# Talking-heads attention, then a Fourier mix with feed-forward: the last Fourier parts placed behind the first feed-forward products

## The chip, the cores and the metric

The kernel runs on one core of one Trainium2 chip. The metric is the device time of one execution in microseconds, median of several runs. Names used below: TensorE (PE, matrix products; its weight load is listed as PEld), VectorE (DVE), ScalarE (ACT), GpSimd (POOL), SyncE (SP, which here only issues transfers). SBUF is the on-chip memory, PSUM the accumulators of TensorE. Each engine works through its own instructions in order and waits where data or a buffer is not ready.

## The reference, cut to what matters

```python
# attention: batch 8, 12 heads, 448 rows, head size 64
scores = scale * np.matmul(q, k.transpose(0, 1, 3, 2))
scores = np.einsum('bhij,hg->bgij', scores, w_pre)      # heads mixed
scores = scores - np.max(scores, axis=-1, keepdims=True)
attn = np.exp(scores)
attn = attn / (np.sum(attn, axis=-1, keepdims=True) + 1e-09)
attn = np.einsum('bhij,hg->bgij', attn, w_post)         # heads mixed again
attn_out = np.matmul(attn, v)
# bridge: (B,H,S,D) -> (B, S, H*D) = (8, 448, 768)
X = np.fft.fft(np.fft.fft(x, axis=1), axis=2)
u = x + np.real(X)
un = (u - mean(u)) / np.sqrt(var(u) + 1e-06)            # over the last axis
ch = np.maximum(un @ w_ch1, 0.0) @ w_ch2                # 768 -> 3072 -> 768
out = u + ch
```

## The kernel before, where it is touched

**Two phases.** `mix_phase` does attention and the Fourier mix batch by batch. Its loop counts steps `s`; a batch has 24 of them, eight batches 192. `ffn_phase` does norm and feed-forward over seven tiles of 512 rows (`t`), for six column blocks of the weights (`c`). One pair (c, t) is called a unit here: `first` makes seven products of w1 (a fast two-by-two scheme with seven instead of eight products), `second` seven of w2. Tile 0 holds the rows of batch 0 and the beginning of batch 1.

**The Fourier mix of a batch** comes behind its attention. `emit_x` turns the attention's output into rows X. `fold` makes sums and differences of pairs of rows on GpSimd. `emit_z` transforms along the rows (TensorE, then a ScalarE copy into z), four times a batch. `emit_s2` transforms along the columns and VectorE adds the result to X, four times a batch. Then `store` writes X to two arrays in DRAM, one of them in reversed order by an indirect transfer. The places of these steps, counted from the batch's first step, run to 55, so for the last batch they lie behind step 192:

```python
AT_X = (11, 20, 24, 29)
AT_Z = (38, 38, 41, 41)
AT_S = ((40, 44), (53, 55))
...
    with tc.manual_schedule(engines={ET.PE, ET.DVE, ET.Activation, ET.Pool}):
        while s < TOT or any(fill.values()):
            ...
            if 0 <= s < TOT:
                emit_turn(s)
            if s >= 4:
                wts.deal(1)
            ...
            for _ in range(min(len(folds), 1 if n and s > 3 else 2)):
                folds.pop(0)()
            take("full", s)          # X, z and s2 that are due
            s += 1
        flush()
        while later:
            later.pop(0)()           # stores
        wts.deal(1000)
```

**The weights** are given as 64-bit numbers. `_Weights` loads a piece raw, rebuilds 32-bit numbers with seven VectorE operations, makes the sums of the fast scheme and stores them. `deal(n)` puts n of these operations into the program. The load of a piece's first raw weight is an operation of its own that counts as none, and the first `deal` of the kernel is that of step 4.

```python
        self.ops.append((lambda: load(k0 + self.ahead - 1), False))
        for k in range(len(ps)):
            self.ops.append((lambda k=k: begin(k), True))
            ...
    def deal(self, n):
        while self.later:
            self.later.pop(0)()
        while self.ops and (n > 0 or not self.ops[0][1]):
            fn, dve = self.ops.pop(0)
            fn()
            n -= dve
```

**The feed-forward phase** begins with its own pools, the loads, the norm of tile 0, and then the units:

```python
    for i in ORDER:
        load_w1(0, i)
    for t in range(2):
        load_u(t)
    for x in range(NT2):
        stats(0, x)              # VectorE
    power(0)                     # four small GpSimd operations: (var + eps) ** -0.5
    for x in range(NT2):
        norm(0, x)               # ScalarE
        turn(0, x)               # six transposes on TensorE, two ScalarE copies
    for n in range(4):
        total(0, n)              # sums for the fast scheme, VectorE
    for i in ORDER:
        load_w2(0, i)
    with tc.manual_schedule(engines={mybir.EngineType.PE, mybir.EngineType.DVE}):
        for n in range(NC * NTB):
            c, t = divmod(n, NTB)
            if c + 1 < NC and t < NK + FM:
                wts.add(c + 1, t)
            wts.deal(0)
            if c == 0 and t + 2 < NTB:
                load_u(t + 2)
            second(n, first(n))
            wts.deal(1000)
```

Its PSUM tiles are two of kind Q and three each of kinds P and R[...].

Of the kernel before, what the change touches and what calls it, by code (L numbers as in the profile page):

```python
# [10 lines left out]
F32 = mybir.dt.float32  # L11
# [270 lines left out]


@with_exitstack
def mix_phase(ctx, tc, ident, q, k, v, w_pre, w_post, u_scr, u_rev, wts):

# [2 lines left out]

    def pool(name, bufs=1, **kw):
        return ctx.enter_context(tc.tile_pool(name=name, bufs=bufs, **kw))

    praw = pool("praw", 4)
    pqt = pool("pqt", 4)
# [4 lines left out]
    psm = pool("psm", 4)  # L301
    ppv = pool("ppv", 2)
    pxt = pool("pxt")
    pxx = pool("pxx", 6)
    pxs = pool("pxs")
    pxf = pool("pxf")
    pzz = pool("pzz")
    wts.open(ctx, tc)
    cst = pool("cst")
    pmx = pool("pmx", space=bass.MemoryType.PSUM)  # L310
# [13 lines left out]
    def room(n):  # L324
        if sum(e[0] for e in pend) + n > 4:
            flush()

    def ms_tile():
        return pms.tile([P, 512], F32, name="ms", tag="ms")


    cn = {n: nc.inline_tensor(a, name="k_" + n) for n, a in _consts().items()}
# [25 lines left out]
                kw2[:, :, r:30:R], wrp[:, 1, :].rearrange("p (y g) -> p y g", y=2),  # L358
                mk[:, 1, r:r + 1], None, op0=ALU.mult)

    rows = cst.tile([PN, 2], U32, name="rows")
    ts = cst.tile([PN, 2, 2, PN], F32, name="ts")
    tcs = cst.tile([CW, 2, 2, 2, DQ + 1], F32, name="tcs")

    def emit_tables():
        for t, n in ((rows, "at"), (ts, "ts"), (tcs, "tc")):
# [312 lines left out]
    def due(kind, at, fn):  # L679
        fill[kind].append((at, len(fill[kind]), fn))  # L680
# [5 lines left out]
    for b in range(B):  # L686
        f = b * GS
        at_t = [(a, nm, xx) for xx, at in enumerate(AT_T) for nm, a in zip("qk", at)]
        for at, (a, nm, xx) in zip(AT_L, sorted(at_t, key=lambda e: e[0])):
            loads.append(f + a - GS)  # L690
            for y in range(2):
                due("none", f + at[y] - GS,
                    lambda b=b, xx=xx, nm=nm, y=y: emit_load_qk(b, xx, nm, y))
        for xx, at in enumerate(AT_T):
            for nm, a in zip("qk", at):
                due("full", f + a - GS, lambda b=b, xx=xx, nm=nm: emit_xpose(b, xx, nm))
        for pr in range(3):
            for y in range(2):
                due("none", f + AT_V[pr][y], lambda b=b, pr=pr, y=y: emit_load_v(b, pr, y))
        for n in range(2 * NG):  # L700
            for xx in range(3):
                due("QK", f + BS * n - 7 + AT_QK[n][xx],
                    lambda n=2 * NG * b + n, xx=xx: (emit_qk(n, xx), n))
        for n in range(NG):
            g = groups[b * NG + n]
            for pr in range(3):
                due("AV", f + GT * (n + 1) + AT_AV[n][pr],
                    lambda g=g, pr=pr: (emit_av(g, pr), None))
            due("full", f + AT_X[n], lambda g=g: emit_x(g))
        for n, at in enumerate(AT_Z):  # L710
            due("full", f + at, lambda b=b, n=n: emit_z(b, n // 2, n % 2))
        for pair in range(2):
            for par in range(2):
                due("full", f + AT_S[pair][par],
                    lambda b=b, pair=pair, par=par: emit_s2(b, pair, par))
    due("none", max(loads[:6]) - 6, emit_load_mix)
    due("none", -3, emit_mix)
    due("none", 3, emit_tables)
# [18 lines left out]
    s = int(min(v_[0][0] for v_ in fill.values()))  # L737
    ET = mybir.EngineType
    with tc.manual_schedule(engines={ET.PE, ET.DVE, ET.Activation, ET.Pool}):
        while s < TOT or any(fill.values()):  # L740
            old = len(later)
            n = take("none", s)
            if 0 <= s + LM < TOT:
                emit_premix(s + LM)
            flush()
            if 0 <= s < TOT:
                emit_postmix(s)
            if 0 <= s + LM < TOT:
                emit_max(s + LM)
                emit_exp(s + LM)  # L750
            take("AV", s)
# [4 lines that stand above are left out]
            take("QK", s)  # L756
            if 0 <= s + LG < TOT:
                if any(e[2] is not None and e[2] <= (s + LG) // BS for e in pend):
                    flush()
                emit_gather(s + LG)  # L760
            if 0 <= s + LM < TOT:
                emit_scale(s + LM)
            for _ in range(old):
                later.pop(0)()
            for _ in range(min(len(folds), 1 if n and s > 3 else 2)):
                folds.pop(0)()
            take("full", s)
            s += 1
        flush()
        while later:  # L770
            later.pop(0)()
        wts.deal(1000)

# [10 lines left out]


@with_exitstack
def ffn_phase(ctx, tc, ident, u_scr, u_rev, wts, ub_scr, out):

    nc = tc.nc

    def pool(name, bufs=1, **kw):
        return ctx.enter_context(
            tc.tile_pool(name=name, bufs=bufs, reuse_waits="tile", **kw))

    pw1 = pool("pw1", 7)
    pub = pool("pub", 11)
    pun = pool("pun", 2)
# [1 line left out]
    ph = pool("ph")  # L801
    pst = pool("pst", 4)
    wts.open(ctx, tc, 2)
    pu = pool("pu")
    pps = pool("pps", space=bass.MemoryType.PSUM)

    NT2 = TB // P
    HT = TB // 2

    def ps_tile(key):  # L810
        return pps.tile([P, 512], F32, name="ps" + key, tag="ps" + key,
                        bufs=2 if key == "Q" else 3)

    us, ubs, w1, w2 = {}, {}, {}, {}
    mhalf = pst.tile([P, NT2], F32, name="mhalf", bufs=1)
    nc.gpsimd.memset(mhalf[:, :], -0.5)

    def load_u(t):
        us[t] = pu.tile([P, NT2, DM], F32, name=f"u{t}", tag=f"u{t}")
        for x in range(NT2):  # L820
            p = 0
            while p < P:
                b, r = divmod(t * TB + x * P + p, S)
                k = sum(r >= e for e in ENDS)
                n = min(P - p, ENDS[k] - r)
                src = (u_rev if k % 2 else u_scr)[b]
                for p0, m in _split(p, n):
                    nc.sync.dma_start(out=us[t][p0:p0 + m, x, :],
                                      in_=src[r + p0 - p:r + p0 - p + m, :])
                p += n  # L830
# [61 lines left out]
    def first(n):  # L892
# [7 lines left out]
        for k, i in enumerate(ORDER):  # L900
# [27 lines left out]
            if norms and k < NT2:  # L928
                stats(t + 1, k)
                if k == NT2 - 1:  # L930
                    power(t + 1)
            if i != 2:
                wts.deal(2 if norms else 3)
            if t == NTB - 1 and c + 1 < NC:
# [10 lines left out]
    def second(n, h):  # L945
# [9 lines left out]
        for k, i in enumerate(ORDER):  # L955
            for x in range(NT2 // 2):
                if i in OPENS:
                    ps[ACC[i], x] = ps_tile(ACC[i])
                p = ps[ACC[i], x][:, :DH]
                for kf in range(FM):  # L960
                    nc.tensor.matmul(p, lhs[i][:, kf, x * P:(x + 1) * P],  # L961
                                     w2[i][:, kf, :], start=i in OPENS and kf == 0,
                                     stop=kf == FM - 1, skip_group_check=True)
                for r, d in {0: [(0, 0)], 1: [(0, 0)], 4: [(1, 1)], 5: [(0, 1)],
                             2: [(0, 1)], 6: [(1, 1)], 3: [(1, 0)]}[i]:
                    us_ = u[:, 2 * r + x, d * DH:(d + 1) * DH]
                    nc.vector.tensor_tensor(us_, us_, p, op=ALU.add)  # L967
                    if c == NC - 1 and i in (1, 6, 2, 3):
                        r0 = t * TB + (2 * r + x) * P
                        nc.sync.dma_start(out=out[r0:r0 + P, d * DH:(d + 1) * DH],  # L970
                                          in_=us_)
            if i == 1:
                nc.vector.tensor_tensor(h12, h12, hs2, op=ALU.subtract)
            if norms and k < NT2:
                turn(t + 1, k)
                if k + 2 < NT2:
                    norm(t + 1, k + 2)
            if norms and k >= NT2 - 1:
                total(t + 1, k - NT2 + 1)
            wts.deal(2 if norms and k >= NT2 else 4)  # L980
            if t == NTB - 1 and c + 1 < NC:
                load_w2(c + 1, i)

    for i in ORDER:
        load_w1(0, i)
    for t in range(2):
        load_u(t)
    for x in range(NT2):
        stats(0, x)
    power(0)  # L990
    for x in range(NT2):
        norm(0, x)
        turn(0, x)
    for n in range(4):
        total(0, n)
    for i in ORDER:
        load_w2(0, i)
    with tc.manual_schedule(engines={mybir.EngineType.PE, mybir.EngineType.DVE}):
        for n in range(NC * NTB):
            c, t = divmod(n, NTB)  # L1000
            if c + 1 < NC and t < NK + FM:
                wts.add(c + 1, t)
            wts.deal(0)
            if c == 0 and t + 2 < NTB:
                load_u(t + 2)
            second(n, first(n))
            wts.deal(1000)


@with_exitstack  # L1010
def kernel(
# [18 lines left out]
    u_rev = [scr.tile([S + 1, DM], F32, name=f"v_{b}") for b in range(B)]  # L1030
    ub_scr = [scr.tile([7, P, NK, TB // 2], F32, name=f"ub_{t}") for t in range(NTB)]
    wts = _Weights(nc, moe_w_ch1, moe_w_ch2, scr)
    mix_phase(tc, ident, q, k, v, w_pre, w_post, u_scr, u_rev, wts)
    ffn_phase(tc, ident, u_scr, u_rev, wts, ub_scr, out.rearrange("b s d -> (b s) d"))


# [29 lines left out]
```

## Time and profile before

| what | value |
|---|---|
| time, median of 3 runs | 2481.18 us (2478.39 to 2484.16) |
| profiled run, span | 2483.8 us, granted TensorE clock 0.987 |
| TensorE busy | 2378.0 us, 96% |
| TensorE weight load busy | 1538.6 us, 62% |
| VectorE busy | 1519.1 us, 61% |
| ScalarE, GpSimd busy | 787.2 us, 778.7 us |
| moved by DMA | 372.09 MB, mean 150 GB/s |

The profile is one execution, recorded instruction by instruction. Its page gives busy time by engine, the span in 40 slices of about 62 us, the chain of work that ended last, and groups of instructions. A busy time says how long an engine had instructions in hand, not how well it used them. An idle time carries a releaser: the instruction, or the transfer, that ended it. Up to about 887 us the kernel is in attention and Fourier mix, where all engines are well loaded; from about 933 us it is in the feed-forward phase, where TensorE is busy nearly without a gap.

### The profile page before, as it was taken

How to read it: one execution, taken by the hardware profiler on the slowest of the kernel's cores; microseconds unless marked ns; L12 is line 12 of the kernel's file. 1: busy time of each engine (PE TensorE's matmuls, PEld its weight loads, DVE VectorE, ACT ScalarE, POOL GpSimd, SP SyncE). 2: the span in 40 equal slices, each digit the busy share in tenths (PEclk: the TensorE clock that was granted, in tenths of full speed). 3: DMA queues.
4: the chain of work that ended last, by engine and by line, in shares of the span. 5: the costliest groups of instructions: out<-in, count | busy, mean ns of one | idle time of the engine just before them, and what ended most of it. 6: DMA issues, size and time to landing. Idle time of an engine off the chain costs nothing.

```text
span 2483.8 us, 48361 instructions
## 1 busy us (share of the span) xinstructions
PE 2378.0 (96%) x18608; PEld 1538.6 (62%) x18608; DVE 1519.1 (61%) x3103; ACT 787.2 (32%) x2059; POOL 778.7 (31%) x1292
## 2 busy tenths in 40 slices
PE   6899999999999949999999999999999999999999
PEld 2344444444444447676777777777777777777776
DVE  3678878788777636786456545754675366533333
ACT  3566666666666513322110111111011111101110
POOL 3477867768675541121011001100110011000000
PEclk9999999999999979999999999999999999999999
DMA  5554555546554446533644354445354535443331
GB/s 136 155 166 157 173 162 170 180 150 187 168 167 139 164 148 208 179 130 124 219 140 145 110 189 129 143 131 182 123 156 131 165 121 155 132 153 117 124 115 51
DMA packets 168579, 372.09 MB, mean 150 GB/s; under 512 B 36734, under 2 KB 90006, under 8 KB 168350
## 3 DMA queue, kind: packets, MB, share of 16 engines
q1 hardware_dynamic: 129038, 260.22, 32.1%
q0 software_dynamic: 33744, 107.40, 14.9%
q8 instruction: 148, 2.42, 0.4%
q10 hardware_dynamic: 5568, 1.38, 0.3%
q14 instruction: 81, 0.66, 0.1%
HBM read 211.98 MB, written 74.34 MB: 115 GB/s over the span
## 4 chain that ended last, share of the span: by engine, by line
PE 82%; DVE 5%; ACT 4%; DMA 4%; POOL 3%; issue 1%; SPq 1%; ACTq 0%; POOLq 0%; DVEq 0%
PE psP L907 18%; PE psP L961 17%; PE psR L907 9%; PE psR L961 9%; PE mx L462 6%; PE psQ L961 4%; PE psQ L907 4%; PE ms L526 4%; PE po L499 4%; ACT PP L478 3%; PE ms L436 3%; DVE nmx L470 3%; DMA Kr<-Sb 2%; PE ms L640 2%; PE ms L624 1%
## 5 line engine op out<-in xcount | busy, mean ns | idle before, releaser
L907 PE MATMUL psP<-ub,w1t 128*128 128x256 f32 x2016 | 462.9, 379 | 0.0
L961 PE MATMUL psP<-w2t,h 128*128 128x384 f32 x1344 | 460.9, 486 | 0.0
L907 PEld LDWEIGHTS psP<-ub,w1t 128*128 128x128 f32 x2016 | 382.8, 190 | 60.7
L207 POOL DMA_DIRECT2D raw<-in_moe_w_ch_dram x120 | 68.9, 574 | 946.9 <-DVE tmp L251 934.1
L961 PEld LDWEIGHTS psP<-w2t,h 128*128 128x128 f32 x1344 | 254.4, 190 | 165.9
L478 ACT ACTIVATE PP<-mx,nmx 128x448 f32<-128x448 f32 x384 | 239.9, 629 | 285.0 <-DVE nmx L470 269.4
L489 POOL TENSOR_SCALAR PP<-PP,rcp 128x448 f32<-128x448 f32 x384 | 240.9, 636 | 272.0 <-DVE rcp L487 228.3
L470 DVE TENSOR_REDUCE nmx<-mx 128x1 f32<-128x448 f32 x384 | 221.4, 618 | 124.5 <-PE mx L462 114.4
L967 DVE TENSOR_TENSOR u<-u,psP 128x384 f32<-128x384 f32 x336 | 183.4, 552 | 143.7 <-PE psP L961 141.5
L912 ACT COPY h<-psP 128x512 f32<-128x512 f32 x42 | 24.6, 585 | 761.7 <-PE psP L907 761.7
L462 PE MATMUL mx<-Kr,kw 60*64 60x448 f32 x1536 | 205.2, 560 | 49.5 <-ACT PP L478 42.2
L907 PE MATMUL psR<-ub,w1t 128*128 128x256 f32 x1008 | 231.4, 379 | 0.0
L961 PE MATMUL psR<-w2t,h 128*128 128x384 f32 x672 | 230.5, 486 | 0.0
L918 DVE TENSOR_TENSOR h<-h,psQ 128x512 f32<-128x512 f32 x42 | 28.9, 688 | 303.6 <-PE psQ L907 303.6
L510 DVE STREAM_TRANSPOSE Pv<-po 128x896 f32<-128x896 f32 x192 | 212.5, 1107 | 3.2 <-PE po L499 3.2
L907 PEld LDWEIGHTS psR<-ub,w1t 128*128 128x128 f32 x1008 | 191.4, 190 | 26.3 <-DVE ub L886 0.3
L499 PE MATMUL po<-PP,kw 60*32 60x448 f32 x3072 | 191.0, 554 | 0.1
L436 PE MATMUL ms<-kT,qT 64*60 64x448 f32 (+1 forms) x1536 | 188.2, 554 | 0.0
L318 ACT COPY Sb<-ms 124x448 f32<-124x448 f32 x384 | 184.6, 540 | 6.1 <-DMA Kr<-Sb 1.6
L526 PEld LDWEIGHTS ms<-Pv,vv 64*64 64x64 f32 x5376 | 142.2, 132 | 68.9 <-issue 30.7
L961 PEld LDWEIGHTS psR<-w2t,h 128*128 128x128 f32 x672 | 127.2, 190 | 87.4
L526 PE MATMUL ms<-Pv,vv 64*64 64x120 f32 x5376 | 164.3, 267 | 0.0
(92 smaller groups left out, 2743.1 us busy)
## 6 DMA issues: line engine op xcount, KB each, us to landing
ub<-ub SPq DMA_DIRECT2D x294, 384.0 KB
Kr<-Sb SPq DMA_DIRECT2D x768, 105.0 KB
raw<-in_moe_w_ch_dram POOLq DMA_DIRECT2D x72, 256.0 KB, 3.4
raw<-in_moe_w_ch_dram POOLq DMA_DIRECT2D x48, 384.0 KB, 3.8
w<-wst POOLq DMA_DIRECT2D x126, 128.0 KB, 3.0
w<-wst POOLq DMA_DIRECT2D x84, 192.0 KB, 2.8
w1t<-w SPq DMA_DIRECT2D x42, 384.0 KB
w2t<-w SPq DMA_DIRECT2D x42, 384.0 KB
```

The costliest lines, as they stand in the source:

```text
L318: (nc.scalar.copy if eng == "a" else nc.vector.tensor_copy)(out=out, in_=in_)
L436: nc.tensor.matmul(pss[x][64 * y:64 * y + r0 + 64 - lo, :S], st["qT", xx][64 * x:64 * x + 64, y, lo:r0 + 64], st["kT", xx][64 * x:64 * x + ...
L462: nc.tensor.matmul(mx[64 * z:64 * z + 64, x, :S], kw1[64 * x:64 * x + KR, :], Kr[64 * x:64 * x + KR, z, :], start=True, stop=True)
L470: nc.vector.tensor_reduce(nmx[:, x:x + 1], steps[T]["mx"][:, x, :S], axis=AX.X, op=ALU.max, negate=True)
L478: nc.scalar.activation(PP[:, x, :], steps[T]["mx"][:, x, :S], ACTF.Exp, bias=steps[T]["nmx"][:, x:x + 1], accum_out=den[:, x:x + 1])
L489: nc.gpsimd.tensor_scalar(PP[:, x, :], PP[:, x, :], rcp[:, x:x + 1], 1.0, op0=ALU.mult, op1=ALU.mult)
L499: nc.tensor.matmul(po[o:o + 32, z, :S], kw2[64 * z:64 * z + KR, y, :], PP[64 * z:64 * z + KR, :, c * HS:(c + 1) * HS], start=True, stop=True)
L510: nc.vector.transpose(g["Pv"][:, T % GT, :].rearrange("p (z s) -> p z s", z=2), steps[T]["po"][:, :, :S])
L526: nc.tensor.matmul(pss[y][64 * x:64 * x + 64, :nu * R], st["v", pr][64 * y:64 * y + 64, x, jb * D:(jb + 1) * D], _ap(Pv, 64 * y * rp + 32 ...
L907: nc.tensor.matmul(p[:, m, :], w1[i][:, kc, m * P:(m + 1) * P], ub[:, kc, :], start=i in OPENS and m == kc == 0, stop=kc == NK - 1, skip_g ...
L961: nc.tensor.matmul(p, lhs[i][:, kf, x * P:(x + 1) * P], w2[i][:, kf, :], start=i in OPENS and kf == 0, stop=kf == FM - 1, skip_group_check ...
L967: nc.vector.tensor_tensor(us_, us_, p, op=ALU.add)
```

## The change

**What it does.** Four things, of which the first three belong together.

1. `mix_phase` ends its loop behind the last X (step 197) and the folds. The Fourier parts that are then still due (one s2 of batch 6; four z and four s2 of batch 7) are returned as a list, and the feed-forward's first unit takes one of them behind each of its products, except behind the products at places 1 and 2 of `first`. The stores of X follow them.
2. The tiles that these parts need (X, folds, z, tables) get pools on the other side of SBUF, that live through the first unit. Two PSUM banks are kept for them during that unit; kinds P and R have two banks each then, and a third one afterwards.
3. The tiles of u are the first pool of the feed-forward phase, so that u0 to u2 lie where raw and transposed q and k were, and the loads of u0 and u1 stand ahead of those of w1. The norm of tile 0 is inside the manual schedule. The first unit does no weight operations: those of the next column block start one unit later.
4. `wts.deal(0)` at step 0 asks for the first raw weight four steps ahead of the `deal` of step 4 that uses it.

It is for filling the joint of the two phases, and the wait for the first raw weight, with other work. The products, sums and transforms themselves are the same.

```diff
+    def late(name, bufs=1):
+        return rest.enter_context(tc.tile_pool(name=name, bufs=bufs, side="right"))
...
-    pxx = pool("pxx", 6)
-    pxs = pool("pxs")
-    pxf = pool("pxf")
-    pzz = pool("pzz")
+    pxx = late("pxx", 6)
+    pxs = late("pxs")
+    pxf = late("pxf")
+    pzz = late("pzz")
+    tbl = late("tbl")
...
+    due("none", 0, lambda: wts.deal(0))
...
-        while s < TOT or any(fill.values()):
+        while s <= TOT - GS + AT_X[-1]:
...
         flush()
+        while folds:
+            folds.pop(0)()
+        wts.deal(1000)
+
+    def part(fn, tile_fn):
         while later:
             later.pop(0)()
-        wts.deal(1000)
+        ms.append(tile_fn)
+        if fn:
+            for e in fn():
+                e()
+
+    return [lambda t, fn=fn: part(fn, t) for _, _, fn in fill["full"] + [(0, 0, None)]]
...
+    pu = [pool("pu")]
     pw1 = pool("pw1", 7)
...
-    pu = pool("pu")
-    pps = pool("pps", space=bass.MemoryType.PSUM)
+    pps = [pool("pps" + k, space=bass.MemoryType.PSUM) for k in "QPR"]
+    beside = ExitStack()
+    ppx = beside.enter_context(
+        tc.tile_pool(name="ppx", bufs=2, space=bass.MemoryType.PSUM))
...
+    def next_part():
+        if parts:
+            parts.pop(0)(lambda: ppx.tile([P, 512], F32, name="ms", tag="ms"))
...
+            if n == 0 and k not in (1, 2):       # in first
+                next_part()
...
+            if n == 0:                           # in second
+                next_part()
...
+    for t in range(2):
+        load_u(t)
     for i in ORDER:
         load_w1(0, i)
-    for t in range(2):
-        load_u(t)
-    for x in range(NT2):
-        stats(0, x)
-    power(0)
...
     with tc.manual_schedule(engines={mybir.EngineType.PE, mybir.EngineType.DVE}):
+        for x in range(NT2):
+            stats(0, x)
+        power(0)
...
-            if c + 1 < NC and t < NK + FM:
-                wts.add(c + 1, t)
+            if c + 1 < NC and 0 <= t - (c == 0) < NK + FM:
+                wts.add(c + 1, t - (c == 0))
...
             second(n, first(n))
             wts.deal(1000)
+            if n == 0:
+                rest.close()
+                pu.append(pool("pu2", side="right"))
+                beside.close()
+                pps.append(pool("ppy", space=bass.MemoryType.PSUM))
```

## Prediction

> **What bounds the kernel now.** I read the page first: TensorE is busy for 96% of 2483.8 us, so only the few slices where it is not can give anything back. Slice 15 of the PE row shows a 4, and the first slice a 6. The stage table shows the same places in numbers (columns: stage; its length; busy us and instructions of PE, weight load, DVE, ACT, POOL; granted clock; DMA share; GB/s).
>
> ```profile
> 62.00:79.00 17.00, 6.76 (x64) 1.61 (x68) 4.42 (x12) 3.93 (x11) 5.30 (x9) 0.71 0.65 170
> 79.00:860.00 781.00, 750.51 (x11684) 359.42 (x11676) 611.88 (x1201) 518.23 (x1570) 555.18 (x892) 1.00 0.52 163
> ...
> 887.00:932.70 45.70, 13.18 (x70) 11.97 (x68) 17.76 (x41) 3.28 (x7) 17.16 (x24) 0.66 0.56 169
> 932.70:977.60 44.90, 43.93 (x189) 32.42 (x190) 29.36 (x65) 17.43 (x30) 7.29 (x14) 0.96 0.60 193
> 977.60:2483.80 1506.20, 1499.50 (x5861) 1102.62 (x5859) 820.25 (x1712) 209.61 (x347) 155.29 (x283) 1.00 0.44 141
> ```
>
> Between attention and feed-forward (887 to 932.7 us) TensorE works 13.2 of 45.7 us, at a clock of 0.66. From 977.6 on only 6.7 us of 1506 are idle, so what is won must come from the joint and the start. Next, the timeline of TensorE and of GpSimd through the joint (start, busy, engine, line, tile, count, and in brackets the idle time before it and its releaser):
>
> ```profile
> 886.36 1.48 PE L640 MATMUL ms<-tcs,z 96*113 96x193 f32 x8
> 898.14 0.69 PE L624 MATMUL ms<-ts,xf 113*97 113x113 f32 x2 [10.30 <-POOL xf L601]
> 907.18 4.18 PE L640 MATMUL ms<-tcs,z 96*112 96x193 f32 x24 [0.62 <-ACT z L318]
> 932.72 2.59 PE L878 MATMUL psQ<-ident,un 128*128 128x128 f32 x10 [21.35 <-ACT un L869]
> ```
>
> ```profile
> 887.18 1.97 POOL L580 TENSOR_TENSOR xs<-X 113x384 f32<-113x384 f32 x2
> 897.10 3.84 POOL L601 TENSOR_TENSOR xf<-xq 113x385 f32<-113x385 f32 x4
> 911.01 0.99 POOL L663 DMA_INDIRECT v<-X,rows  x1 [10.07 <-DVE X L653]
> 929.56 0.25 POOL L858 TENSOR_SCALAR mv<-mv 128x4 f32<-128x4 f32 x1 [13.34 <-DVE mv L854]
> 929.89 1.05 POOL L859 TENSOR_TENSOR mv<-mv,mhalf 128x4 f32<-128x4 f32 x1
> ```
>
> TensorE waits twice. First 10.3 us for the folds of the last pair of rows on GpSimd. Then 21.35 us for the tail: additions to X, the scatter of reversed rows, the loading of u behind it on the same SyncE queue, statistics, and four small GpSimd operations of the norm. Yet u0 consists of batches 0 and 1, stored long ago: the wait is one of order, not of data.
>
> The chain of work and the VectorE timeline at the start:
>
> ```profile
> 62.47 9.69 DMA raw<-in_moe_w_ch_dram
> ```
>
> ```profile
> 72.18 0.29 DVE L229 TENSOR_SCALAR tmp<-raw 128x256 uint32<-128x256 uint32 x1 [10.23 <-DMA raw<-in_moe_w_ch_dram]
> ```
>
> The first raw weight is asked for in the step that uses it. It takes 9.7 us behind the Fourier tables, VectorE waits 10.2 us, and TensorE 9.8 us (75.31, waiting for the exponential behind that VectorE).
>
> **What the Trainium skill says.** "Perfetto Trace Analysis", section Optimization Strategy, says that a kernel with regimes bound by different engines can gain from interleaving them; the trace agrees that there is something to interleave: the tail has a TensorE of 29% beside a GpSimd chain, the feed-forward one of 99.6%. "TensorE: Matmul & The Clock Gate", section What's actually happening, gives half clock after an idle window of about 3.4 us and full clock after as much work. The trace fits: 16 matmuls of the mixing take 1.74 us at 77.01, after the 9.8 us gap, and 0.98 us otherwise; the joint has 0.66. "DMA: Bandwidth & Descriptors", section Issuing engines are not separate DMA queues, says that all queues share the 16 engines. The trace agrees: in 60 to 70 us the share is 0.84 to 0.88 and all landings become slow (v rows 9.1 us, tables 9.0, raw 9.8, against about 3 to 4 elsewhere). This matters for the start.
>
> **The change part by part.** The instruction order of the changed program shows: after the last transposes into X come the 24 transposes of u0, then each of the first unit's products with one of the nine remaining Fourier parts behind it (four z, five s2). No arithmetic is added; it is moved.
>
> (1) When can the norm of u0 start? The loads of u0 stand among the last gathers on SyncE, and statistics of u0 right after the last turn on VectorE (877 us), so both are early. But the program's order on GpSimd puts the square-root power of u0's norm behind all folds. Those begin when X is copied at 887.1 us (ACT 886.23 plus 0.86). From the trace: pairs 1.97, sides 1.0, quarters 1.14 + 0.13, twice = 8.5; four sums 3.84; two raw-weight issues of 0.56 among them = 1.1; the first norm operation 0.25; gaps of about 0.1 each, some 0.6. Against that, one indirect store (1.0) that stood among them now stands behind. Folds end near 887.1 + 14.3 = 901.4, about as now (900.9). Then 1.05 + 0.2 + 0.3 plus 0.2 of gaps: the norm's activation starts at about 903 instead of 931.64. That is 28.6 us earlier.
>
> (2) From the activation to the end of the first product group (i = 0) the kernel before takes 940.25 - 931.64 = 8.6 us, with half of that group already between the transposes. In the new order the group stands wholly behind the transposes: these end 7.3 us after the activation (938.96), and the group takes 2.6, so 9.9. Loss 1.3 us.
>
> (3) The Fourier parts now use time in which TensorE was otherwise full. Two z of 16 matmuls take 1.72 us (the chain, 841.07), one s2 of 8 takes 1.49 to 1.56. Four z = 3.4, five s2 = 7.6, sum 11.0 us.
>
> (4) Waits inside the first unit. VectorE gets 20 additions of 0.47 us (9.4), but loses the 32 weight operations of this unit (0.24 to 0.43 each, about 11), which move one unit later. The one tight place is z01: its ScalarE copy stands behind two norm activations of u1 (2 x 1.03), which wait for statistics and power: about 7.3 us after the Q product ends, and TensorE reaches the s2 that needs it 7.0 us after. Two P accumulators instead of three: the second of the feed-forward's second half waits for one ScalarE relu of 0.6, behind which a z and the first P product stand. I allow 1 us in all.
>
> (5) w1 now lies where Sb and the transposed q and k were, w2 where Pv was (free after the last product with V at 884.3). From 871 on 1.6 MB of u1, 2.75 MB of w1, then 2.75 MB of w2 must land; at the 0.2 MB per us of 60 to 70 us w1 is there by 895, w2 by 910. They are needed from 910 and 937. Nothing.
>
> Joint: 28.6 - 1.3 - 11.0 - 1 = 15.3 us.
>
> (6) Start. The raw weight, "four steps ahead", is asked for at about 46.7 us behind the q loads, so VectorE finds it at step 4. But the product with V of step 6 then comes up soon: one step lasts 3.8 us (58.64 to 62.43), so it would start at about 68.1 rather than 78.69. It needs the second half of v's first rows, issued at 61.79 and landing 9.1 us later, 70.9 to 71.5, behind the same tables. So the wait goes over to v: TensorE starts there at about 71.5. Gain 78.69 - 71.5 = 7.2 us, not 10.6.
>
> (7) From the second unit on the weights of the next column block are one unit later, but still inside the seven units of the first block; accumulators are three again. No change.
>
> Sum: 15.3 + 7.2 = 22.5 us. Predicted time 2481.2 - 22.5 = 2458.7, say 2459 us, 0.9% faster.
>
> **The rivals.** (A) The joint gains all it idles: 31.7 us there, and 10.6 at the start, so about 2439. For it speaks that u0 has no dependence on the tail. Against it: the power operation behind the folds on GpSimd, which keeps TensorE idle from about 888 to 904 still; and v behind the tables. (B) The interleaving costs more than it hides: the parts and the products share in-order ACT and DVE queues, and each part that waits for a z copy stops the whole product stream. Nine parts at 1 to 2 us would eat the joint's gain, leaving about 2470. For it: the z01 order above. Against: most copies have one or two product groups of 2.6 us as slack. (C) The loading of u0 amid the last gathers, on one SyncE queue, delays the attention's last steps: the gathers are four steps ahead (15 us), and the kernel before had seven w1 loads of 384 KB in the same place, so I give it at most 2 us. (D) The raw weight's wait is wholly replaced by v's or the gathers': only 3 us gained at the start, 2463.
>
> **Range and chances.** The terms that are uncertain: start of the norm (2 us), stalls inside the unit (3), landing of v (3), measurement (3 of 2478 to 2484). Together some 5 to 6 us to either side; for the unknown I widen it to 2449 to 2469. A gain above 2% would need 2431.6, more than all idle time at both places recovers; a loss above 2% needs 50 us of new waits. So 0.02, 0.96, 0.02.
>
> **What would show it.** Right: TensorE's transposes of u0 begin at about 897 (904 less the 7 of the start) released by the norm's ScalarE activation, itself by GpSimd; the idle time before them is some 16 us; the first unit lasts about 51 us from its first product, 11 more than the next; near 66 us TensorE waits for v for about 3 us and no VectorE wait for raw remains. Wrong: a norm that comes before the folds (then rival A), gaps between the first unit's products of more than 2 us in sum (B), ScalarE or TensorE waiting on gathers in the last steps (C), or product groups that wait for w1 or w2.

## The result, and the profile after

The changed kernel takes 2461.76 us (median of four runs, 2458.43 to 2465.96); the kernel before, run beside it, 2479.78 (2477.29 to 2484.16). The ratio is 0.9926, with an interval of 0.9905 to 0.9948: 0.7% faster, less than the 2% from which a kernel is called faster here. The prediction was 2459 us, its range 2449 to 2469.

The work is the same: TensorE is busy for 2373.4 us (2378.0 before), VectorE for 1518.6 (1519.1), with the same number of instructions. Most of the gain is idle time: 19.1 of the 23.7 us between the two profiled spans. The stage table of the kernel after, from inside the one wait to the end of the first unit (stage; length; busy us and instructions of PE, weight load, DVE, ACT, POOL; granted clock; DMA share; GB/s):

```profile
884.00:895.80 11.80, 0.00 (x0) 0.00 (x0) 0.48 (x2) 0.15 (x1) 11.12 (x18) 0.50 0.59 200
895.80:908.40 12.60, 11.15 (x44) 9.18 (x45) 4.79 (x7) 7.70 (x13) 0.00 (x0) 0.60 0.46 179
908.40:953.60 45.20, 45.09 (x218) 34.99 (x217) 27.12 (x52) 12.66 (x22) 4.82 (x7) 1.00 0.36 120
```

From 908.4 us TensorE has no idle time worth a name; the two waits of the kernel before (10.3 and 21.35 us) are one now, and in the part of it that the table shows GpSimd works 11.12 of 11.8 us. After it come 12.6 us at a clock of 0.60.

For all kernels below I cut the trace at five events: the first product of post-mixing (`po<-PP`) of step 4 and that of step 8; the end of the last copy that makes X (ScalarE); the first norm activation of u0; the first product of the second unit. In the profiled runs, in us:

| stage | before | after |
|---|---|---|
| start: step 4 to step 8 (15.2 where nothing waits: four steps of 3.8) | 26.34 | 21.72 |
| attention: step 8 to last copy of X | 801.20 | 798.78 |
| last copy of X to norm of u0 | 44.55 | 15.23 |
| norm of u0 to second unit | 45.93 | 57.97 |
| second unit and all after | 1506.23 | 1506.48 |

In the last row the second unit itself has 39.86 in both. The joint (rows three and four) went from 90.48 to 73.20, 17.3 us less; the start gave 4.6, and attention, whose code the change leaves alone, 2.4. That is 24.3, less 0.25 at the end and 0.4 ahead of step 4: the 23.7 between the two spans (2483.8 and 2460.1). The medians differ by 18.0.

TensorE through the joint (start, busy, engine, line, tile, count, and in brackets the idle time before and its releaser):

```profile
896.73 3.01 PE L912 MATMUL psQ<-ident,un 128*128 128x128 f32 x12 [16.88 <-ACT un L903]
900.13 3.22 PE L912 MATMUL psQ<-ident,un 128*128 128x128 f32 x12 [0.39 <-ACT ub L914]
903.14 4.14 PE L941 MATMUL psP<-ub,w1t 128*128 128x256 f32 x12
907.12 1.47 PE L648 MATMUL ms<-tcs,z 96*113 96x193 f32 x8
908.43 2.75 PE L941 MATMUL psR<-ub,w1t 128*128 128x256 f32 x12
...
916.20 0.94 PE L632 MATMUL ms<-ts,xf 113*97 113x113 f32 x8
916.98 2.77 PE L941 MATMUL psP<-ub,w1t 128*128 128x256 f32 x12
```

One wait is left, 16.88 us, ended by the norm. Behind it 24 transposes and the first product group run slowly (4.14 us for the twelve matmuls that later take 2.75), and then each Fourier part (L648 and L632) stands between two products with no idle time in brackets; it goes on so up to the second unit at 953.62.

What the norm waits for is on GpSimd (first fence), and on VectorE (second):

```profile
890.15 3.84 POOL L609 TENSOR_TENSOR xf<-xq 113x385 f32<-113x385 f32 x4
893.95 1.05 POOL L893 TENSOR_TENSOR mv<-mv,mhalf 128x4 f32<-128x4 f32 x1
```

```profile
877.80 1.02 DVE L887 BATCH_NORM_STATS2 st<-u 128x6 f32<-128x384 f32 x2 [8.77 <-PE ms L534]
```

The power of the norm (893.95) runs as soon as the last fold (890.15, 3.84 us) is through: between the two GpSimd has no gap. The statistics of u0 were held up too, by 8.77 us, and not by u0: the releaser is the last product with V. The small statistics tile lies where Pv was; stats_free and stats_late below put it elsewhere.

The start, on TensorE:

```profile
66.78 0.96 PE L470 MATMUL mx<-Kr,kw 60*64 60x448 f32 x2 [0.88 <-ACT PP L486]
69.70 2.28 PE L470 MATMUL mx<-Kr,kw 60*64 60x448 f32 x6 [1.96 <-DMA Kr<-Sb]
71.92 1.52 PE L507 MATMUL po<-PP,kw 60*32 60x448 f32 x16
73.37 1.69 PE L534 MATMUL ms<-Pv,vv 64*64 64x120 f32 x56
```

VectorE has no wait for the raw weight any more (its first operation on it begins at 62.24, after none). But the pre-mixing stops for 1.96 us for a gather (Kr, the scores in another layout), in the midst of its eight matmuls, and the six that remain take 2.28 us, where eight take 0.98 at full clock. The product with V begins at 73.37.

### The profile page after: what moved, and what is told of

It is laid out like the page before. It is cut to its first block, busy times and chain, and to the rows that moved or that the text cites. A ratio compares the mean times of both kernels' runs of the same rounds, so it can differ in the third digit from the quotient of the medians.

```text
span 2460.1 us, 48351 instructions
## 1 busy us (share of the span) xinstructions
PE 2373.4 (96%) x18608; PEld 1536.8 (62%) x18608; DVE 1518.6 (62%) x3103; ACT 787.0 (32%) x2059; POOL 779.9 (32%) x1292
## 4 chain that ended last, share of the span: by engine, by line
PE 84%; DVE 5%; ACT 4%; DMA 3%; POOL 2%; issue 1%; SPq 1%; ACTq 0%; POOLq 0%; DVEq 0%
PE psP L941 18%; PE psP L997 18%; PE psR L941 9%; PE psR L997 9%; PE mx L470 6%; PE ms L534 5%; PE psQ L997 4%; PE psQ L941 4%; PE po L507 4%; ACT PP L486 3%; PE ms L444 3%; DVE nmx L478 3%; DMA Kr<-Sb 2%; PE ms L648 2%; PE ms L632 1%
```

## The experiments

Twelve runs, in three groups; each stood beside the kernel before on the same chip, and all ratios are to that.

| kernel | median us (before) | ratio, interval | start | attention | X to norm | norm to second unit |
|---|---|---|---|---|---|---|
| start_only | 2476.27 (2484.03) | 0.9970, 0.9958 to 0.9982 | 21.50 | 798.76 | 44.17 | 47.29 |
| joint_only | 2469.66 (2484.03) | 0.9943, 0.9929 to 0.9957 | 27.18 | 798.35 | 15.26 | 57.99 |
| tables_later | 2462.37 (2484.03) | 0.9909, 0.9893 to 0.9924 | 15.57 | 806.77 | 15.26 | 57.99 |
| tables_only | 2482.10 (2484.03) | 0.9987, 0.9979 to 0.9995 | 20.54 | 804.97 | 43.13 | 46.79 |
| norm_ahead | 2462.94 (2484.91) | 0.9907, 0.9892 to 0.9922 | 22.48 | 807.04 | 12.09 | 56.01 |
| stats_free | 2451.92 (2484.91) | 0.9863, 0.9848 to 0.9878 | 23.14 | 812.93 | -4.29 | 57.55 |
| parts_first | 2467.76 (2484.91) | 0.9931, 0.9918 to 0.9945 | 20.34 | 808.57 | 15.23 | 63.09 |
| tables_spread | 2461.43 (2484.91) | 0.9907, 0.9891 to 0.9922 | 15.44 | 805.49 | 15.23 | 56.01 |
| after_again | 2469.21 (2487.78) | 0.9924, 0.9908 to 0.9940 | 23.60 | 805.40 | 15.27 | 58.09 |
| stats_late | 2450.39 (2487.78) | 0.9859, 0.9840 to 0.9878 | 19.06 | 807.34 | -3.40 | 56.66 |
| both | 2444.22 (2487.78) | 0.9831, 0.9814 to 0.9848 | 15.56 | 807.70 | -3.40 | 56.66 |
| weights_first_unit | 2469.23 (2487.78) | 0.9931, 0.9915 to 0.9947 | 21.68 | 802.51 | 15.27 | 60.62 |

How far can this table be trusted? The unchanged kernel after, run again, has the same ratio (0.9924 to 0.9926) and the same joint (73.36 to 73.20), but 6.6 us more of attention. Attention has a spread of up to 10 us between kernels whose attention code is equal (798.35 to 808.57); so a stage is compared with the same stage, and a span is not used as proof of a few us. The start varies too: seven kernels with the same start code (after, norm_ahead, stats_free, parts_first, after_again, stats_late, weights_first_unit) took 19.06 to 23.60 us there.

> The changed kernel itself once more, so that the variants beside it have it on the same chip: 17 to 21 us below the kernel before.

### Which part gives what

start_only is the kernel before with one line more; joint_only is the kernel after without it.

```diff
+    due("none", 0, lambda: wts.deal(0))
```

> The kernel before with one line added: the first raw weight is asked for at step 0. Theory 1 (the wait is only partly won, because the product with V and the gathers of step 6 then wait for transfers in the crowd of the Fourier tables): TensorE reaches the first product with V near 73 us instead of 78.7, the time falls by 4 to 5 us, and TensorE waits some 2 to 3 us for a gather or for v near 67 us. Rival (the raw wait is the whole loss, nothing takes its place): 10 us less.

> The changed kernel without the early request for the first raw weight. Theory (the joint gives 29.3 earlier start of the norm, less 2.9 for the transposes and the first product at half clock, less 9.1 for the Fourier parts): about 17 us below the kernel before, and from the end of the last copy into X to the first product of the second unit 73 us instead of 90.5. Rival (most of the 18 us comes from the start of the kernel): 8 to 10 us below.

The start alone takes its stage from 26.34 to 21.50; the joint alone takes the joint from 90.48 to 73.25, and leaves the start at 27.18. In the kernel after, which has both, the stages are 21.72 and 73.20: each part gives in its own stage nearly the same with and without the other, and the joint gives the larger share. By the medians they are worth 7.8 and 14.4 us, together 22.1, where the kernel after has 18.0 and 18.6; the intervals are too wide to tell these apart. The 7.8 of start_only is more than the 4 to 5 expected, and more than its stage shows (4.8).

What stops the start is the same in start_only as in the kernel after. TensorE in start_only:

```profile
72.01 1.63 PE L462 MATMUL mx<-Kr,kw 60*64 60x448 f32 x6 [2.54 <-DMA Kr<-Sb]
73.57 1.74 PE L499 MATMUL po<-PP,kw 60*32 60x448 f32 x16
```

TensorE waits 2.54 us for the gather, and the post-mixing behind it runs at half clock (1.74 for 0.98).

### What delays the start: the burst of tables

If the Fourier tables (0.78 MB in one burst) make the raw weight and the gather late, they must both be early once the tables are elsewhere. tables_later is the kernel after, tables_only the kernel before, each with

```diff
-    due("none", 3, emit_tables)
+    due("none", 20, emit_tables)
```

> The changed kernel with the three Fourier tables (0.78 MB) asked for at step 20 instead of step 3; they are first used at step 38. Theory 1 (tables crowd the transfers of 57 to 72 us): the waits near 67 us vanish, the first product with V starts near 68 us, 5 us earlier than in the changed kernel (73.4), and the time falls by another 4 to 6 us. Rival (v and the gathers are late by themselves): no change, TensorE still waits near 67 us.

> The kernel before with only the tables moved to step 20; the raw weight is still asked for in the step that uses it. Theory 1: the raw weight lands in about 4 us instead of 9.7, VectorE waits some 4 us instead of 10.2, and the time falls by 6 to 8 us: the order of the tables alone is worth as much as the early request. Rival (the late request is what costs, whatever else is in the queue): at most 2 us less.

In tables_later the start takes 15.57 us, as if nothing waited. But the burst strikes at its new place. TensorE of tables_later, at the start and at step 20:

```profile
69.67 1.70 PE L534 MATMUL ms<-Pv,vv 64*64 64x120 f32 x56
...
134.54 1.75 PE L470 MATMUL mx<-Kr,kw 60*64 60x448 f32 x2 [2.82 <-DMA Kr<-Sb]
...
137.90 3.08 PE L534 MATMUL ms<-Pv,vv 64*64 64x120 f32 x56
```

Again a wait for a gather, 2.82 us, then half clock (3.08 for 1.70). The DMA share there is 0.78 (126 to 136 us); at the start in the kernel after it is 0.89 (60 to 70 us). Attention is 8.0 us longer than in the kernel after; how much of it is this one place, the profile doesn't say, since the spread is as large. The median is 21.7 us below the kernel before, where the kernel after has 18.0 and 18.6; the further 4 to 6 us that were expected don't stand clear of the intervals.

tables_only shows what the line of the change does and the tables don't. VectorE of tables_only:

```profile
67.02 0.29 DVE L229 TENSOR_SCALAR tmp<-raw 128x256 uint32<-128x256 uint32 x1 [3.72 <-DMA raw<-in_moe_w_ch_dram]
```

The raw weight lands 4.6 us after its issue instead of 9.7, yet, asked for in the step that uses it, it still costs 3.72 us of VectorE's time. Of the wait of 10.2 us before, the tables made about 6.5. The start's stage falls by 5.8 us (26.34 to 20.54), but the time by only 1.9, where 6 to 8 were expected: in this kernel too the burst strikes at its new place, with a wait of 3.04 us for a gather at 139.57 us, and attention is 3.8 us longer than before, which is within its spread.

tables_spread divides the tables into six pieces, with no transfer over 198 KB, at steps of their own:

```diff
-    due("none", 3, emit_tables)
+    for i, at in enumerate((9, 18, 10, 11, 16, 17)):
+        due("none", at, lambda i=i: emit_tables(i))
```

> The changed kernel with the Fourier tables asked for in six pieces of at most 198 KB, at the steps 9, 10, 11, 16, 17, 18 in which no q, k or v is loaded, instead of all at step 3 (and instead of all at step 20, where they held up a gather by 2.8 us and TensorE at half clock behind it). Theory (a burst of transfers delays a gather wherever it stands; pieces don't): no wait over 1 us near 67 us and none at steps 9 to 18, about 6 us below the changed kernel. Rival (the bytes cost the same wherever they are): same time as the changed kernel, with small gather waits spread over steps 9 to 18.

The start is 15.44 us, 6 to 8 less than in the kernel after (21.72 and 23.60), and from 60 to 130 us TensorE waits for no gather (one of 0.95 us comes at 132). The median does not show it plainly (0.9907 against 0.9924 to 0.9926, intervals overlapping); with the statistics moved besides, it does: see "both". In this run TensorE waited longest for a gather elsewhere, where no table is loaded. TensorE of tables_spread:

```profile
261.43 0.96 PE L474 MATMUL mx<-Kr,kw 60*64 60x448 f32 x2 [2.33 <-DMA Kr<-Sb]
262.33 1.74 PE L511 MATMUL po<-PP,kw 60*32 60x448 f32 x16
```

So late gathers are not made by the tables alone; they come up at other places in other runs. What made this one late isn't shown. Nor do they explain attention's spread: over the whole stage TensorE waits 3.1 us for gathers in joint_only (798.35 us) and only 2.2 in after_again (805.40). It is busy for 762.8 and 769.2 us there, for the same work: the larger part of the difference is matmuls that ran slower. Why they did so in one run and not in the other stays open.

### What delays the norm: the order on GpSimd, and a tile's place

norm_ahead is the kernel after with the folds behind the norm's power in the program:

```diff
-        while folds:
-            folds.pop(0)()
         wts.deal(1000)
...
         power(0)
+        while folds:
+            folds.pop(0)()
```

> The changed kernel with the folds of the last rows written behind the norm's power instead of ahead of it, so that on GpSimd the power stands among the folds. Theory (the power's place behind the folds holds the joint): the norm's ScalarE activation starts about 3 us earlier, 12 us after the last copy into X instead of 15.2, and the time falls by about 3 us. Rival (the loads of u0 or the statistics hold it): the activation starts 15 us after the copy as before, no change.

The norm begins 12.09 us after the last copy of X instead of 15.23: only 3.1 us earlier than in the kernel after. GpSimd and VectorE of norm_ahead:

```profile
897.68 0.99 POOL L593 TENSOR_TENSOR xs<-xs 113x383 f32<-113x383 f32 x1
898.63 1.05 POOL L891 TENSOR_TENSOR mv<-mv,mhalf 128x4 f32<-128x4 f32 x1
```

```profile
885.47 1.02 DVE L885 BATCH_NORM_STATS2 st<-u 128x6 f32<-128x384 f32 x2 [8.68 <-PE ms L534]
```

The folds still run around the norm's operations, and VectorE still waits 8.68 us for the last product with V before it makes the first statistics. So the place of the folds in the program is worth little as long as the statistics are late. The joint as a whole is 5.3 us shorter than in after_again (68.10 to 73.36): 3.2 to the norm, and 2.1 behind it. The 2.1 are not the folds' doing. tables_spread, whose joint is that of the kernel after, has the same 56.01 us behind the norm. There too TensorE came to full clock early, behind the same wait of 16.88 us. TensorE of tables_spread:

```profile
900.88 0.93 PE L917 MATMUL psQ<-ident,un 128*128 128x128 f32 x6 [0.39 <-ACT ub L919]
903.32 2.75 PE L946 MATMUL psP<-ub,w1t 128*128 128x256 f32 x12
```

How long the half clock lasts behind this wait differs from run to run (12 transposes in 3.22 us and the product group in 4.14 in the kernel after), so 2 us of a joint can be chance.

stats_free gives the statistics tile memory that is free long before (where raw q and k were); the folds stay as in norm_ahead:

```diff
     pu = [pool("pu")]
+    pst = pool("pst", 4)
     pw1 = pool("pw1", 7)
...
-    pst = pool("pst", 4)
```

> As the one with folds behind the power, and the small tiles of the statistics get the pool right behind u's, where q and k were, so that the statistics of u0 no longer wait for the memory of the last products with V. Theory: statistics and power are done before the last rows of attention, the transposes of u0 follow the last transposes into X at once, the 16.9 us gap of TensorE goes to under 3, and the time is 12 to 17 us below the changed kernel, near 2447. Rival 1 (the weights w1 are then not there): the gap is filled by a wait for w1, 5 to 8 us gained. Rival 2 (statistics amid attention's last steps hold up VectorE): attention ends 3 to 5 us later and eats part of it.

The norm now begins 4.29 us before the last copy of X, and the joint falls to 53.26 us: 14.8 below norm_ahead, 19.9 below the kernel after. This is where the rest of the joint's wait was, once the power no longer stood behind the folds; the tile's new place with the folds left ahead of the power was not run. It has a price. VectorE and TensorE of stats_free:

```profile
860.14 1.02 DVE L885 BATCH_NORM_STATS2 st<-u 128x6 f32<-128x384 f32 x2 [4.05 <-DMA u<-v]
```

```profile
863.93 1.77 PE L470 MATMUL mx<-Kr,kw 60*64 60x448 f32 x8 [5.78 <-ACT PP L486]
```

With nothing to hold them, the statistics stand earlier in VectorE's order than u0's load has landed; VectorE, in order, waits 4.05 us, and TensorE, four attention steps from the end, 5.78 us behind it.

stats_late puts the tile where PP, the probabilities, was, which comes free with the last post-mixing (by the layout of the pools; its pool follows `pub` instead of `pu`):

```diff
     pub = pool("pub", 11)
+    pst = pool("pst", 4)
     pun = pool("pun", 2)
```

> The changed kernel with the folds behind the norm's power, and the small tiles of the statistics where the attention weights PP were: these come free before the last products with V, but only with the last steps, so that the statistics of u0 stand behind the last turn on VectorE and not amid the steps. Theory (the joint's remaining 16.9 us is held by order and memory alone; in the variant with the statistics where q and k were, attention lost some 4 to 5 us because VectorE waited 4.05 us for u0): from the last copy into X to the second unit about 54 us as there, instead of 73.2, with no new wait in the last steps; the time 16 to 19 us below the changed kernel, near 2446. Rival (the weights w1, or the clock after the last steps, then hold the first products): 8 us or less.

The joint is again 53.26 us, 20.1 below after_again on the same chip, and the first statistics have no wait. VectorE, then TensorE of stats_late, in the last steps and at the joint:

```profile
874.37 0.98 DVE L885 BATCH_NORM_STATS2 st<-u 128x6 f32<-128x384 f32 x2
```

```profile
860.06 1.77 PE L470 MATMUL mx<-Kr,kw 60*64 60x448 f32 x8 [1.13 <-ACT PP L486]
...
885.54 0.71 PE L910 MATMUL psQ<-ident,un 128*128 128x128 f32 x5
...
891.50 2.76 PE L939 MATMUL psP<-ub,w1t 128*128 128x256 f32 x12
```

The transposes of u0 begin at 885.54, amid those into X; the wait of 16.88 us is gone, and the first product group runs at full clock (2.76 us). The late statistics no longer stop attention. That the ratios of stats_free (0.9863) and stats_late (0.9859) agree means that the 5.78 us are hidden in attention's spread, or partly made good; I can't tell which.

### Are the parts better behind products than in one row?

parts_first is the kernel after with all Fourier parts ahead of the first product:

```diff
+            while parts:
+                next_part()
             second(n, first(n))
```

> The changed kernel with all nine Fourier parts in one row right behind the transposes of u0 and ahead of the first product, instead of one behind each product; the early norm stays. Theory (dealing out hides the parts' ScalarE copies and additions behind products): in a row the parts take about 13 us instead of 9.7, so 3 to 5 us slower than the changed kernel. Rival (only the early norm counts, the dealing out is worth nothing): within 1 us of the changed kernel.

TensorE of parts_first:

```profile
915.90 1.25 PE L632 MATMUL ms<-ts,xf 113*97 113x113 f32 x8
917.77 1.02 PE L632 MATMUL ms<-ts,xf 113*96 113x113 f32 x8 [0.62 <-ACT z L324]
```

The joint is 78.32 us, 5.0 more than in after_again. The parts take 15.7 us in a row (913.33 to 929.07), more than the 13 expected: five waits of 0.62 to 0.82 stand among them, three of them for a ScalarE copy of z, 3.3 us in sum. Put behind products, the same parts have none. So the larger part of the joint's gain is the early norm, and the dealing out is worth about 5 us.

### Is the weights' shift needed?

weights_first_unit takes the one-unit shift back, so that the first unit has its 32 weight operations again beside the additions of the parts:

```diff
-            if c + 1 < NC and 0 <= t - (c == 0) < NK + FM:
-                wts.add(c + 1, t - (c == 0))
+            if c + 1 < NC and t < NK + FM:
+                wts.add(c + 1, t)
```

> The changed kernel with the weight operations of the next column block starting in the first unit again, as in the kernel before (32 VectorE operations, about 11 us, beside the 20 additions of the Fourier parts). Theory (VectorE has room in the first unit: it is busy for about 35 of 58 us): within 2 us of the changed kernel, the first unit at most 1 us longer. Rival (the additions and the weights together delay the evictions, so the shift was needed): the first unit 3 us or more longer.

TensorE of weights_first_unit, near the end of the first unit:

```profile
948.39 1.01 PE L912 MATMUL psQ<-ident,un 128*128 128x128 f32 x6 [1.31 <-DVE u L1003]
```

TensorE waits 1.31 us here, and 1.40 at the second unit's first product, for VectorE's additions that free an accumulator, 2.7 us in sum, and the joint is 2.5 us longer (75.89 to 73.36). So VectorE had less room than the theory gave it (at most 1 us longer). The medians (2469.23 and 2469.21) don't show the difference. In the joint of this pair the shift is worth about 2.5 us.

### The two improvements together

"both" is stats_late with the spread tables.

> The one with late statistics, and the Fourier tables in six pieces besides. Theory: the gains add, as they lie at different places: 6 us at the start, of which single late gathers elsewhere may take back a part (with pieces alone one run had such a gather near 259 us): 18 to 25 us below the changed kernel, 2440 to 2446. Rival (the bytes of the tables cost the same anywhere): same as the one without pieces, within 2 us.

2444.22 us (2442.68 to 2447.99), ratio 0.9831 (0.9814 to 0.9848): 25 us below the kernel after on the same chip, and below the kernel before by 1.7%. It is 6.2 us below stats_late (2448.92 to 2454.32); the two ranges don't touch. The start (15.56 us to 19.06) explains 3.5 of it in the profiled pair. The 19.06 are the shortest start of the seven kernels without this step; both kernels with spread tables have 15.4 to 15.6.

## Why the prediction was right, step by step

The sum was 22.5 us (15.3 and 7.2); the stages of the profiled pair show 21.9 (17.3 and 4.6), the medians 18.0, with 12.9 to 23.6 from the ratio's interval. The terms are less good than the sum: the start was put too high by 2.6 us and the joint too low by 2.0, and these cancel. The mechanism was right in the main; that the sum comes so close to the stages' is luck.

**(1) The norm's earlier start: right, with a cause left out.** Predicted 28.6 us, measured 44.55 - 15.23 = 29.3. The power does run directly behind the folds. But "statistics of u0 right after the last turn on VectorE (877 us), so both are early" failed: VectorE waited 8.77 us for memory of Pv. In this kernel it hid behind the folds. It mattered for what could still be won: norm_ahead, which I would have thought the remedy from this step, gained 3.1 us of these 15, and the tile's place another 15 to 16 (12.09 to -3.40 or -4.29).

**(2) The first product group: mis-sized.** From the norm's activation to the group's end 907.12 - 895.65 = 11.5 us, not 9.9; the loss was 2.9, not 1.3. I gave the group 2.6 us, as if the transposes ahead of it had brought the clock to full. It took 4.14. The Trainium skill, "TensorE: Matmul & The Clock Gate", section What's actually happening, says that full clock comes after about 3.4 us of sustained work. The runs show this and a longer time too. In the kernel after some 9 us passed, through transposes with a pause of 0.39, and in joint_only, tables_later, after_again and weights_first_unit the group took 4.10 to 4.27 too. In tables_spread and norm_ahead full clock was there 3.4 us after the first transpose, and the term measured 9.5 us, near the 9.9. So the missing 1.6 us of this term vary from run to run; what decides it stays open.

**(3) Cost of the Fourier parts: somewhat too high.** From start to start in the row of TensorE one s2 takes 908.43 - 907.12 = 1.31 us and one z 916.98 - 916.20 = 0.78: five and four make 9.7 instead of 11.0. I had used busy times, of which those of neighbouring groups overlap.

**(4) Waits in the first unit: none, where I allowed 1 us.** z01, "the one tight place", did not stop TensorE. The kernel before had two waits there itself, 0.24 and 0.32 us. From the first product of kind R to the second unit it took 37.38 us, now 45.19; with the s2 just ahead (1.31) the parts cost 9.1 us net. weights_first_unit shows what the shift does for VectorE there: without it TensorE waits 2.7 us. So the joint is 29.3 - 2.9 - 9.1 = 17.3.

**(5) Landing of w1 and w2: right.** No product waits for them.

**(6) The start: the mechanism half right, the size too large.** Predicted 7.2 us, measured 4.6 (with the spread of the start, 2.7 to 8.1 for a kernel before and a kernel with this start code). "The wait goes over to v" failed as put: it went to a gather first, at 67.7 us, on another queue but behind the same tables. The half clock after it (2.28, 1.52 us) takes the product with V to 73.37, not 71.5. The cause, the tables, was right: with the tables spread the start has no such wait. The Trainium skill, "DMA: Bandwidth & Descriptors", section Queues, rings and completion order, says that each transfer engine takes the queues it has work for in turn, packet by packet. That fits a gather on SyncE's queue that is slowed by a burst on GpSimd's, with the share at 0.89; that the turns are what delays it, no run shows.

**(7) Later units: right.** Second unit 39.86 us in both; from it to the end 1506.23 and 1506.48.

**The rivals.** A fell: 16.88 us of idle time remain, for the reason given there. But stats_late shows that they could be had. B fell: no gaps between products. C did not show in the kernel after: attention is not longer, and TensorE waits for no gather in the last steps, though the gap of 2.13 us described at the end stands among them. It came true in stats_free, where the statistics wait for u0's load inside attention. D (3 us at the start) named the gathers rightly; the stage lies between it and my 7.2.

**The marks.** Transposes at 896.73 (897 predicted) after 16.88 us of idle time (16), released by the norm; the first unit 953.62 - 903.14 = 50.5 us (51), 10.6 more than the next (11). The one that failed is the 3 us wait for v.

## What to carry to other kernels

When work of one phase is moved across a joint, look for waits that are of order or of memory rather than of data: here a small tile of statistics, placed under a large one that is in use to the end, held back the norm that the whole joint waited for, and this cost nothing visible while a longer queue hid it. Moving it, with the folds behind the power, was worth more than the change's whole dealing-out, and memory that comes free too early was no better than a place that orders the instruction rightly. A burst of bulk transfers, here 0.78 MB, is best divided and put where no small, urgent transfer is due; moved as a whole, it took its wait along in both kernels tried.

## What was not expected of the hardware

**Half clock behind short waits, but not behind all.** Waits of 1.96, 2.54 and 2.82 us for a gather were each followed by some us of TensorE at about half clock (16 post-mixing matmuls 1.52 to 1.74 us instead of 0.98). The Trainium skill, "TensorE: Matmul & The Clock Gate", section What's actually happening, puts the fall after an idle window of about 3.4 us; here the waits were shorter. In after_again the pre-mixing at 64.02 us ran at half clock (1.74 us for eight) with no longer wait ahead of it than 0.99. The kernel before has such places too, so the prediction's "0.98 us otherwise" was read too narrowly:

```profile
860.94 1.74 PE L499 MATMUL po<-PP,kw 60*32 60x448 f32 x16
```

The wait ahead of it is 1.90 us. But in stats_free the post-mixing at 878.03 us took 0.99 behind a wait of 1.90, and the kernel after stays at full clock behind the 2.13 us below. So the length of the last wait does not decide it alone; what does, no run shows.

**A gap with no releaser.** In every kernel with the new joint TensorE stops 2.0 to 2.7 us amid the last products with V, at a point where the kernels with the old joint don't. TensorE of the kernel after:

```profile
876.60 1.09 PE L534 MATMUL ms<-Pv,vv 64*64 64x120 f32 x33 [2.13 <-issue]
```

"issue" means that the profile shows nothing waited for. During this gap (874.47 to 876.60 us) the DMA share is full (1.01), as loads of u and of weights land there; in the kernel before TensorE passes the same place without a stop at a share of 0.03 (880.0 to 884.2 us). It lies inside attention's stage, so it is not in the terms above. Whether the transfers make it stays open: no run was aimed at it.
